# Where LayerNorm rows run and when filler steps are issued beside sliding-window attention

## The chip, the cores and the metric

One core of a Trainium2 chip runs the whole program. The metric is the device time of one execution in microseconds (us). The engines are TensorE (PE, its weight loads shown apart as PEld), VectorE (DVE), ScalarE (ACT), GpSimd (POOL), and SyncE (SP), on whose queue nearly all DMAs are issued.

## The reference

A transformer block whose two LayerNorms are modulated by a condition: sliding-window attention, then a dense network with the mish activation, each with a gated residual. All is fp32. There are 2048 tokens of width D = 448, 16 heads of Dh = 28, a window W = 256 and a hidden width F = 1792.

```python
mod = (silu(c) @ w_mod).reshape(1, 6, 1, 448)
sa, ca, ga, sb, cb, gb = (mod[:, i] for i in range(6))
h = layernorm(x) * (1 + ca) + sa
q, k, v = split_heads(h @ wqkv)                       # 16 heads of 28
scores = q @ k.T * 28 ** -0.5
mask = (i - j >= 0) & (i - j < 256)                   # query i, key j
o = softmax(where(mask, scores, -1e9)) @ v
x = x + ga * (merge_heads(o) @ wo)
h = layernorm(x) * (1 + cb) + sb
x = x + gb * (mish(h @ w1 + b1) @ w2)                 # mish: t * tanh(log1p(exp(t)))
```

## The kernel before

**Arithmetic.** An fp32 value that TensorE multiplies is split into a high part, written by ScalarE as a rounded copy, and a low part, the value minus that copy, written by VectorE or GpSimd. A product is then three matmuls: high with high, high with low and low with high.

**Tiling.** The tokens are cut into 4 groups (0 to 3) of 512. A group and a head make a slot, 64 in all (`s`), and a slot has three attention units (`BLOCKS`); the unit number `u` runs from 0 to 191, 48 to a group. A name such as `P58` in an order is that of unit 58.

**One unit of attention.** `B` puts the scores of keys against queries into a PSUM bank (`sB`, L709 and L720) and lets ScalarE take the exponential twice: `P` in fp32 (L723) and `Ph`, the high part (L724). `SP` lets GpSimd make the low part, `Pl` = P - Ph (L731). `PV` multiplies both by the values into `pv` (L741), `Ph` two units later and `Pl` three. The row maximum that the exponential needs comes earlier: `A` computes scores the other way round (`sA`, L679), VectorE reduces each to a maximum (`mx`, L681), and for each pair of slots `M2` turns the maxima and splits them (`mr`, L689 and L690), and a DMA adds them to the queries as further rows. `sA`, `sB`, `pv` and `mm` (for filler) have two PSUM banks each, P, Ph and Pl three buffers each.

**After attention.** `EV` copies a finished slot out of PSUM on ScalarE: `o` (L747) and `ol` (L749). For every four slots (a quad) `QA` adds the two on GpSimd, `T1` turns the sum on VectorE into `t4` and takes the reciprocal `rc` of the softmax denominators (L770), `TM` multiplies by it on GpSimd (L775), and `T2` turns the result back on VectorE into `on` (L779). When four quads are there, the group's output is complete and `on_full` holds the group.

**Filler.** Between the units of a group, `fill_main` issues work of neighbouring groups. In group g (for g over 0) it finishes the q and k projections of group g, waits until `on_full` holds group g-1, and issues `gen_oT` (high part of `on` on ScalarE, L621, low part on VectorE) and `gen_wo` (the output projection, with the residual and the statistics of LN2 behind it). Then `gen_hT` for group g+1 turns the normalized rows through TensorE (four turnings, `tr`), and modulates them into a high part (ScalarE) and a low part (VectorE), and `gen_qkv` projects them. How much of it goes to a unit is set by credit: each unit adds `RATE[g]`, and each filler step takes off what it yields (for matmuls about their share of time, for a turning a constant).

**Side work.** Once in a unit `side_step` advances a second list: above all LN1 of the next group (`gen_ln` with a key that begins with a: statistics `mva` on VectorE, `rsa`, 1 / sqrt(variance + eps), on GpSimd with L233 and L234, then four rows `xin` of 128 tokens, L240, with `dup` on GpSimd behind each), sums for the modulation, and loading of the FFN's weights. LN2 uses the same `gen_ln` with keys f0 to f3 and its rows, `x1`, on VectorE; f0 is issued in the last units of attention.

**Order.** The order on each engine is the order in which the program issues; each engine takes its instructions strictly in turn. `Pipe` holds back stages of a filler item: `add(hold, f1, f2)` calls f1 at the next step, f2 at the one after, and None stands for a step without work. `later` is a queue of DMAs, from which a step takes one at most. After the last unit (`u` = 192 and on) the FFN runs, with L923 (`z`) and L1114 to L1116 (`acc`) as its matmuls; it takes the span from about 440 us.

Of the kernel before, what the change touches and what calls it, by code (L numbers as in the profile page):

```python
# [51 lines left out]
def adaln_block(ctx: ExitStack, tc: tile.TileContext, x, wqkv, wo, w1, b1, w2, c, w_mod, out):  # L52
    nc = tc.nc
    PE, ACT, DVE, POOL = nc.tensor, nc.scalar, nc.vector, nc.gpsimd
# [36 lines left out]
    def bank(tag, bufs, name):  # L91
        return PS[0].tile([128, 512], F32, name=name, tag=tag, bufs=bufs)
# [32 lines left out]
    for part in range(3):  # L125
        for ci in range(4):
            r0, r1 = ci * 128, min(ci * 128 + 128, D)
            for h in ((slice(0, 128),) if ci < 3 else (slice(0, 64), slice(64, 128))):
                t = wqs[ci][h]
# [87 lines left out]
    def ln_stats(x, mv, pl, key):  # L217
        st = pl.tile([128, 6], F32, name=f"st{key}", tag="st", bufs=2)
        DVE.bn_stats(st, x)
        DVE.bn_aggr(mv, st)  # L220

    def dup(x):
        POOL.tensor_copy(x[:, D:512], x[:, 384:448])

    def gen_ln(tiles, pl, xn_tiles, key, mv=None):
        if mv is None:
            mv = pl.tile([128, 4, 2], F32, name=f"mv{key}", tag="mv", bufs=2)
            for t in range(4):
                ln_stats(tiles[t], mv[:, t, :], pl, f"{key}{t}")
                if t < 3:  # L230
                    yield
        rs = pl.tile([128, 4], F32, name=f"rs{key}", tag="rs", bufs=2)
        POOL.tensor_scalar(rs, mv[:, :, 1], EPS, None, op0=ALU.add)  # L233
        POOL.tensor_tensor(rs, rs, mhalf, op=ALU.pow)  # L234
        yield
        yield
        xs = xn_tiles()
        for t in range(4):
            xn = xs[t]
            (POOL if key[0] == "a" else DVE).tensor_scalar(xn[:, 0:D], tiles[t], mv[:, t, 0:1], rs[:, t:t + 1],  # L240
                                                           op0=ALU.subtract, op1=ALU.mult)
            if t:
                dup(xs[t - 1])
            yield xs
        dup(xs[3])

    def tr_chunk(xs, ci, p):
        for t in range(4):
            PE.transpose(p[:, t * 128:(t + 1) * 128], xs[t][:, ci * 128:(ci + 1) * 128], ident)  # L249
# [5 lines left out]
    def hT_hi(p, ci, hh, si):  # L255
        ACT.activation(hh[:, ci], p, AF.Identity, scale=cols[:, si + 1, ci:ci + 1], bias=cols[:, si, ci:ci + 1])

    def hT_lo(p, ci, hh, hl, si, y=True):
        if y:
            hT_y(p, ci, si)  # L260
        DVE.tensor_tensor(hl[:, ci], p, hh[:, ci].bitcast(F32), op=ALU.subtract)

    def new_T(key, pl):
        return (pl.tile([128, 4, GT], F32R, name=f"hh{key}", tag="hh"),
                pl.tile([128, 4, GT], F32R, name=f"hl{key}", tag="hl"))
# [17 lines left out]
    pipe = Pipe()  # L283
    ht_done = set()

    def gen_hT(g):
        drain(ln1[g])
        hh, hl = HT[g] = new_T(g, mid)
        for ci in range(4):
            p = bank("mm", 2, f"tr{g}{ci}")  # L290
            tr_chunk(XS[g], ci, p)
            pipe.add(2, lambda p=p, ci=ci: hT_hi(p, ci, hh, 0), lambda p=p, ci=ci: hT_lo(p, ci, hh, hl, 0))
            yield 1.2
        ht_done.add(g)
        if g + 1 < NG:
            loads = (lambda: x_load(g + 1),) if g > 1 else (lambda: (x_tile(g + 1), x_half(g + 1, 0)),
                                                            lambda: x_half(g + 1, 2))
            pipe.add(0, None, None, lambda: later.extend(loads))
# [5 lines left out]
    def drain(*gs):  # L304
        for g in gs:
            for _ in g:
                pipe.step()
# [17 lines left out]
    def flush():  # L325
        while later:
            later.pop(0)()
# [289 lines left out]
    def gen_oT(g, oT_pool):  # L617
        o = on[g]
        oh, ol = OT[g] = new_T(f"o{g}", oT_pool)
        for ci in range(4):  # L620
            ACT.activation(oh[:, ci], o[:, ci], AF.Copy)  # L621
            pipe.add(1, lambda ci=ci: DVE.tensor_tensor(ol[:, ci], o[:, ci], oh[:, ci].bitcast(F32), op=ALU.subtract))
            if ci < 3:
                later.append(lambda t=ci: xr_load(g, t))
            yield
        yield
        if g == NG - 1:
            yield
# [36 lines left out]
    NS = NG * H  # L665
# [78 lines left out]
    def EV(i, part):  # L744
        a = i % 4 * 32
        if part == 0:
            ACT.activation(O4[a:a + 32], pvb[i][0:32, :], AF.Copy)  # L747
        elif i < NS - 3:
            ACT.activation(OL4[a:a + DH], pvb[i][32:60, :], AF.Copy)  # L749
        else:  # L750
            DVE.tensor_copy(OL4[a:a + DH], pvb[i][32:60, :])

    def quad(qd):
        g, ci = divmod(qd, 4)
        if ci == 0 and g not in on:
            on[g] = mid.tile([128, 4, GT], F32, name=f"on{g}", tag="on")
        return on[g][:, ci], T4.rearrange("p (b d) -> p b d", d=32)
# [14 lines left out]
    def TM(qd):  # L772
        o, t = quad(qd)
        for eng, a, b in ((POOL, 0, 16),) if qd < NS // 4 - 1 else ((POOL, 0, 6), (DVE, 6, 16)):
            eng.tensor_tensor(t[:, a:b, 0:28], t[:, a:b, 0:28], rcq[qd][:, a:b].to_broadcast([128, b - a, 28]), op=ALU.mult)  # L775

    def T2(qd):
        o, t = quad(qd)
        DVE.transpose(o, T4)  # L779
        if qd % 4 == 3:  # L780
            on_full.add(qd // 4)
# [204 lines left out]
        if not (told.get(g) == "bank" and pipe.held() or told.get(g) in taken):  # L986
            told[g] = next(side[g], None)

    RATE = {0: 0.56, 1: 0.91, 2: 0.91, 3: 0.65}
    FRONT = {0: 0, 1: 2, 2: 2, 3: 2}  # L990
    ln1 = {g: gen_ln1(g) for g in range(1, NG)}
    fillers = {g: fill_main(g) for g in range(NG)}
# [2 lines left out]
    def step(g):  # L995
        return next(fillers[g], 99.0) or RATE[g]

# [37 lines left out]
    NU = 3 * NS  # L1035
    credit = 0.0
    for u in range(NU + 9):
        s, k = divmod(u, 3)
        g = s // H
        if k == 0 and s % H == 0 and 0 < g < NG:  # L1040
            drain(fillers[g - 1], side[g - 1])
            flush()
        pipe.step()
        if 0 <= u - 3 < NU:
            PV(u - 3, Pl)
            if k == 2 and s % 4 != 1:
                EV(s - 1, 0)
        if k == 0 and 0 <= s - 2 < NS:
            if s % 4 == 2:
                EV(s - 2, 0)  # L1050
            EV(s - 2, 1)
        qd = (s - 5) // 4
        if k == 1 and s % 4 == 1 and 0 <= qd < NS // 4:
            QA(qd)
        if u < NU:
            B(u)
        if 0 <= u - 1 < NU:
            SP(u - 1)
        a = s + LEAD
        if a < NS:  # L1060
            A(a, (0, 1, 3)[k])
        if k == s % 2 and s < NS:
            load_slot(s + LEAD + 2)
        if k == 2 and s % 4 == 1 and 0 <= qd < NS // 4:
            T1(qd)
            TM(qd)
        qd = (s - 6) // 4
        if k == (1 if u < NU else 0) and s % 4 == 2 and 0 <= qd < NS // 4:
            T2(qd)
        if g < NG:  # L1070
            v = u - 48 * g
            if v in (0, 12):
                chunk["v"] = 4 if v == 0 and g or 0 < g < NG - 1 else 2
            if v == 0:
                credit = 0.0
            credit += RATE[g] * (2 if v < FRONT[g] else 1)
            while credit > 0.0:
                credit -= step(g)
        if k == 0 and (a - 1) % 2 == 1 and LEAD <= a - 1 < NS:
            M2((a - 1) // 2)  # L1080
        if g < NG:
            if v > 1 or g == 0:
# [12 lines left out]
        if 0 <= u - 2 < NU:
            PV(u - 2, Ph)
# [53 lines left out]
    for n in range(NN + 1):  # L1150
        g, f = divmod(n, NF)
# [44 lines left out]
```

## Time and profile before

| | |
|---|---|
| time, median of 3 runs | 728.78 us (727.71 to 729.55) |
| the profiled execution | 728.02 us, of which 726.2 are the profile's span |
| mean granted TensorE clock | 0.979 |
| busy: PE, DVE, ACT, POOL | 689.5, 397.5, 422.5, 368.9 us |
| issued DMA data | 83.74 MB |

The span starts with the program's first instruction and ends with its last. A group's line gives: source line, engine and operation, output<-inputs, count, then busy time and the mean in ns of one, and behind the second bar the idle time of the engine just before these instructions with what ended it. In the timeline a line gives start, duration, engine, line, operation, and in brackets the wait and what released it. Names lose their numbers there: `P` is any unit's. The granted clock of 1.00 is full speed.

### The profile page before, as it was taken

What the parts mean: (1) busy time and instruction counts of PE and PEld (TensorE: products, weight loads), DVE (VectorE), ACT (ScalarE), POOL (GpSimd) and SP (SyncE); (2) the same over time, 40 slices, a digit from 0 to 9 for tenths busy, and PEclk for the clock granted to TensorE, in tenths of its full rate; (3) what the DMA queues carried; (4) which work ended last, traced back from release to release, by engine and by line L of the source; (5) the groups of instructions that cost most, each with busy time, mean ns of one, the idle gap of its engine ahead of it and who ended that gap; (6) DMA issues with size and microseconds to landing.
All of it is one profiled execution on the core that took longest, in us unless ns stands there. A gap on an engine that the chain in (4) does not pass through costs nothing. (4 is left out here: it accounts for less than half of the span.)

```text
span 726.2 us, 11790 instructions
## 1 busy us (share of the span) xinstructions
PE 689.5 (95%) x3873; PEld 586.1 (81%) x3873; DVE 397.5 (55%) x992; ACT 422.5 (58%) x772; POOL 368.9 (51%) x369
## 2 busy tenths in 40 slices
PE   8998999889999899999899899999999999999996
PEld 8776777678888687888687678888888888888885
DVE  5677767757765958676868776232324133323112
ACT  4549888768877868778978894334233222322221
POOL 7576888797765897677779847332010000000002
PEclk9999999989999999999989899999999999999999
DMA  7855863444482452664764155500200030001001
GB/s 217 258 200 176 247 200 116 137 132 158 135 261 68 150 181 95 171 193 124 227 189 129 52 172 158 141 14 1 101 1 1 0 102 1 0 1 51 0 1 51
DMA packets 48329, 83.74 MB, mean 115 GB/s; under 512 B 6286, under 2 KB 26428, under 8 KB 48268
## 3 DMA queue, kind: packets, MB, share of 16 engines
q1 hardware_dynamic: 47804, 82.98, 36.7%
q8 instruction: 31, 0.51, 0.3%
q14 instruction: 30, 0.25, 0.1%
q10 hardware_dynamic: 464, 0.00, 0.0%
HBM read 53.34 MB, written 29.36 MB: 114 GB/s over the span
## 5 line engine op out<-in xcount | busy, mean ns | idle before, releaser
L731 POOL TENSOR_TENSOR Pl<-P,Ph 128x512 fp32r<-128x512 f32 (+2 forms) x192 | 235.6, 1238 | 66.3 <-ACT Ph L724 39.1
L681 DVE CUSTOM_DVE_ANT_0 junk<-sA,mask 128x384 bf16<-128x384 f32 (+2 forms) x256 | 134.4, 525 | 93.6 <-PE sA L679 84.6
L929 ACT ACTIVATE t<-z,b1c 128x512 f32<-128x512 f32 x56 | 38.5, 687 | 190.5 <-PE z L923 187.4
L931 DVE TENSOR_TENSOR al<-t,ah 128x512 fp32r<-128x512 f32 x56 | 40.7, 726 | 188.3 <-ACT ah L930 188.3
L723 ACT ACTIVATE P<-sB 128x512 f32<-128x512 f32 (+2 forms) x192 | 110.0, 573 | 43.4 <-PE sB L720 36.1
L679 PE MATMUL sA<-k,q 84*128 84x384 f32 (+2 forms) x256 | 103.9, 408 | 8.2 <-DVE mx L681 5.2
L724 ACT ACTIVATE Ph<-sB 128x512 fp32r<-128x512 f32 (+2 forms) x192 | 109.3, 569 | 0.0
L923 PE MATMUL z<-hhf,w 128*128 128x512 f32 x224 | 89.4, 399 | 0.0
L741 PE MATMUL pv<-Pl,v 128*60 128x256 f32 (+2 forms) x352 | 76.7, 293 | 12.8 <-POOL Pl L731 12.0
L923 PE MATMUL z<-hlf,w 128*128 128x512 f32 x224 | 88.4, 395 | 0.0
L1115 PE MATMUL acc<-w2l,ah 128*128 128x448 f32 x224 | 81.6, 364 | 0.4 <-POOL w2l L893 0.4
L1114 PE MATMUL acc<-w2h,ah 128*128 128x448 f32 x224 | 81.8, 365 | 0.0
L1116 PE MATMUL acc<-w2h,al 128*128 128x448 f32 x224 | 81.7, 365 | 0.0
L741 PE MATMUL pv<-Ph,v 128*60 128x256 f32 (+2 forms) x352 | 79.2, 300 | 0.0
L709 PE MATMUL sB<-q,k 86*128 86x256 f32 (+1 forms) x352 | 76.8, 293 | 2.1 <-ACT Ph L724 1.4
L709 PEld LDWEIGHTS sB<-q,k 86*128 86x128 f32 x352 | 63.5, 196 | 5.1 <-ACT Ph L724 2.2
L923 PE MATMUL z<-hhf,w1l 128*128 128x512 f32 x168 | 66.3, 395 | 0.0
L741 PEld LDWEIGHTS pv<-Pl,v 128*60 128x60 f32 x352 | 45.4, 136 | 24.7 <-POOL Pl L731 18.3
L679 PEld LDWEIGHTS sA<-k,q 84*128 84x128 f32 x256 | 50.8, 200 | 15.5 <-DVE mx L681 9.2
L720 PE MATMUL sB<-fdmask,identr 128*128 128x128 bf16 (+1 forms) x320 | 61.7, 259 | 0.0
L1123 POOL TENSOR_TENSOR yo<-yo,x 128x448 f32<-128x448 f32 (+1 forms) x4 | 4.2, 1058 | 108.1 <-DVE yo L1120 108.1
L741 PEld LDWEIGHTS pv<-Ph,v 128*60 128x60 f32 x352 | 47.4, 137 | 14.3 <-issue 1.3
(155 smaller groups left out, 1337.0 us busy)
## 6 DMA issues: line engine op xcount, KB each, us to landing
scr<-st SPq DMA_DIRECT2D x24, 512.0 KB
k<-scr SPq DMA_DIRECT2D x48, 252.0 KB
q<-scr SPq DMA_DIRECT2D x64, 168.0 KB
scr<-st SPq DMA_DIRECT2D x32, 256.0 KB
x<-x1d SPq DMA_DIRECT2D x10, 448.0 KB
xin<-in_A_x_dram SPq DMA_DIRECT2D x8, 448.0 KB
xr<-in_A_x_dram SPq DMA_DIRECT2D x16, 224.0 KB
x1d<-xr SPq DMA_DIRECT2D x16, 224.0 KB
```

The costliest lines, as they stand in the source:

```text
L679: PE.matmul(p[:, c0:384], q[0:84, t * 128:(t + 1) * 128], k[0:84, t * 128 + c0:t * 128 + 384], start=True, stop=True)
L681: DVE.tensor_tensor_reduce(out=junk[:, c0:384], in0=p[:, c0:384], in1=mask[:, c0:384], scale=1.0, scalar=-3.0e38, op0=ALU.add, op1=ALU.max ...
L709: PE.matmul(p[:, c:c + 128 * (t1 - t0)], k[:, jj * 128:(jj + 1) * 128], q[:, t0 * 128:t1 * 128], start=(n == 0), stop=False, skip_group_ch ...
L720: PE.matmul(p[:, c:c + n], identr, fdmask[:, m:m + n], start=False, stop=True, skip_group_check=True)
L723: ACT.activation(P[:, c0:], p[:, c0:], AF.Exp, scale=SCALE)
L724: ACT.activation(Ph[u][:, c0:], p[:, c0:], AF.Exp, scale=SCALE)
L731: eng.tensor_tensor(Pl[u][:, a:b], Pt[u][:, a:b], Ph[u][:, a:b].bitcast(F32), op=ALU.subtract)
L741: PE.matmul(pv[0:60, t0 * 128:t1 * 128], V[j % NV][:, h, :], P[u][:, c:c + 128 * (t1 - t0)], start=(P is Ph and b == 0 and n == 0), stop=F ...
L923: PE.matmul(zb[n], ps[m][1], ps[m][0], start=(m == 0), stop=(m == 10))
L1114: PE.matmul(p, ah[n][:, ts], w2h[f], start=(f == 0), stop=False)
L1115: PE.matmul(p, ah[n][:, ts], w2l[f], start=False, stop=False)
L1116: PE.matmul(p, al[n][:, ts], w2h[f], start=False, stop=(f == NF - 1))
```

## The change

Five things change.

1. The rows of LN1 in groups 1 to 3 (`xin`, twelve of 128 x 448) are normalized by ScalarE as `Identity(rs * x + nm)` instead of by GpSimd as `(x - mean) * rs`. GpSimd makes the bias nm = -mean * rs with two more small operations behind `rsa`.
2. For the keys a1, a2, a3 and f0 the rows are issued one unit later (one more `yield`).
3. A turning in `gen_hT` takes 1.9 off the credit instead of 1.2, and the credit per unit grows: `RATE` from 0.56 to 0.64 in group 0, from 0.91 to 1.02 in groups 1 and 2.
4. The low part of `gen_oT` (VectorE) is issued one step later.
5. The division `TM` moves from behind `T1`, the third unit of its slot, to the first unit of the next slot, and `T2` from the second unit of that slot to the third.

```diff
         POOL.tensor_tensor(rs, rs, mhalf, op=ALU.pow)
+        if key[0] == "a":
+            nm = pl.tile([128, 4], F32, name=f"nm{key}", tag="nm", bufs=2)
+            POOL.tensor_scalar(nm, mv[:, :, 0], -1.0, None, op0=ALU.mult)
+            POOL.tensor_tensor(nm, nm, rs, op=ALU.mult)
         yield
         yield
+        if key in ("a1", "a2", "a3", "f0"):
+            yield
         xs = xn_tiles()
         for t in range(4):
             xn = xs[t]
-            (POOL if key[0] == "a" else DVE).tensor_scalar(xn[:, 0:D], tiles[t], mv[:, t, 0:1], rs[:, t:t + 1],
-                                                           op0=ALU.subtract, op1=ALU.mult)
+            if key[0] == "a":
+                ACT.activation(xn[:, 0:D], tiles[t], AF.Identity, scale=rs[:, t:t + 1], bias=nm[:, t:t + 1])
+            else:
+                DVE.tensor_scalar(xn[:, 0:D], tiles[t], mv[:, t, 0:1], rs[:, t:t + 1],
+                                  op0=ALU.subtract, op1=ALU.mult)
...
             pipe.add(2, lambda p=p, ci=ci: hT_hi(p, ci, hh, 0), lambda p=p, ci=ci: hT_lo(p, ci, hh, hl, 0))
-            yield 1.2
+            yield 1.9
...
             ACT.activation(oh[:, ci], o[:, ci], AF.Copy)
-            pipe.add(1, lambda ci=ci: DVE.tensor_tensor(ol[:, ci], o[:, ci], oh[:, ci].bitcast(F32), op=ALU.subtract))
+            pipe.add(2, None, lambda ci=ci: DVE.tensor_tensor(ol[:, ci], o[:, ci], oh[:, ci].bitcast(F32), op=ALU.subtract))
...
-    RATE = {0: 0.56, 1: 0.91, 2: 0.91, 3: 0.65}
+    RATE = {0: 0.64, 1: 1.02, 2: 1.02, 3: 0.65}
...
         if k == 2 and s % 4 == 1 and 0 <= qd < NS // 4:
             T1(qd)
-            TM(qd)
         qd = (s - 6) // 4
-        if k == (1 if u < NU else 0) and s % 4 == 2 and 0 <= qd < NS // 4:
-            T2(qd)
+        if s % 4 == 2 and 0 <= qd < NS // 4:
+            if k == 0:
+                TM(qd)
+            if k == (2 if u < NU else 0):
+                T2(qd)
```

In the changed kernel the lines of the attention stand nine further down (L723 becomes L732, L731 becomes L740); the rows are L247 on ScalarE and L249 on VectorE.

**ScalarE, early in group 1 (units 58 to 60).** `xin2` are rows of LN1 for group 2, `hho0` the high parts of group 0's attention output, `o4` and `ol4` a slot's copy out of PSUM. Before:

```order
L723 ACTIVATE P58_2137<-sB58_2133 128x512
L724 ACTIVATE Ph58_2138<-sB58_2133 128x512
L621 ACTIVATE hho0_2069<-on0_1026 128x512
L747 ACTIVATE o4_462<-pv18_2098 32x512
L723 ACTIVATE P59_2165<-sB59_2160 128x512
L724 ACTIVATE Ph59_2166<-sB59_2160 128x512
L749 ACTIVATE ol4_463<-pv18_2098 28x512
L723 ACTIVATE P60_2189<-sB60_2184 128x512
L724 ACTIVATE Ph60_2190<-sB60_2184 128x512
```

Now:

```order
L732 ACTIVATE P58_2139<-sB58_2135 128x512
L733 ACTIVATE Ph58_2140<-sB58_2135 128x512
L630 ACTIVATE hho0_2099<-on0_1020 128x512
L756 ACTIVATE o4_462<-pv18_2102 32x512
L732 ACTIVATE P59_2167<-sB59_2162 128x512
L733 ACTIVATE Ph59_2168<-sB59_2162 128x512
L630 ACTIVATE hho0_2099<-on0_1020 128x512
L247 ACTIVATE xin2_1114<-xin2_1114,nma2_2054,rsa2_2051 128x448
L758 ACTIVATE ol4_463<-pv18_2102 28x512
L732 ACTIVATE P60_2192<-sB60_2187 128x512
L733 ACTIVATE Ph60_2193<-sB60_2187 128x512
L247 ACTIVATE xin2_1114<-xin2_1114,nma2_2054,rsa2_2051 128x448
```

A high part of the attention output and the first row now stand between Ph59 and P60, and the second row between Ph60 and P61.

**GpSimd at the same place (units 53 to 57).** `t4` is the division of a quad, `Pl53` to `Pl57` the low parts of units 53 to 57. Before:

```order
L775 TENSOR_TENSOR t4_464<-t4_464,rc3_2008 128x16x28
L731 TENSOR_TENSOR Pl53_2037<-P53_1998,Ph53_1999 128x512
L233 TENSOR_SCALAR rsa2_2047<-mva2_1918 128x4
L234 TENSOR_TENSOR rsa2_2047<-rsa2_2047,mhalf_136 128x4
L731 TENSOR_TENSOR Pl54_2063<-P54_2033,Ph54_2034 128x512
L731 TENSOR_TENSOR Pl55_2092<-P55_2059,Ph55_2060 128x512
L731 TENSOR_TENSOR Pl56_2114<-P56_2088,Ph56_2089 128x512
L240 TENSOR_SCALAR xin2_1100<-xin2_1100,mva2_1918,rsa2_2047 128x448
L731 TENSOR_TENSOR Pl57_2141<-P57_2110,Ph57_2111 128x512
```

Now:

```order
L740 TENSOR_TENSOR Pl53_2040<-P53_2006,Ph53_2007 128x512
L784 TENSOR_TENSOR t4_464<-t4_464,rc3_2016 128x16x28
L233 TENSOR_SCALAR rsa2_2051<-mva2_1922 128x4
L234 TENSOR_TENSOR rsa2_2051<-rsa2_2051,mhalf_136 128x4
L237 TENSOR_SCALAR nma2_2054<-mva2_1922 128x4
L238 TENSOR_TENSOR nma2_2054<-nma2_2054,rsa2_2051 128x4
L740 TENSOR_TENSOR Pl54_2069<-P54_2036,Ph54_2037 128x512
L740 TENSOR_TENSOR Pl55_2093<-P55_2065,Ph55_2066 128x512
L740 TENSOR_TENSOR Pl56_2117<-P56_2089,Ph56_2090 128x512
L740 TENSOR_TENSOR Pl57_2143<-P57_2113,Ph57_2114 128x512
```

The division stands behind Pl53 instead of ahead of it, two operations on 4 elements stand ahead of Pl54, and no row stands ahead of Pl57.

**VectorE late in group 3 (LN2 of group 0 begins).** `mx62` are row maxima of slot 62, `mr30` the turned and split maxima of an earlier pair, `x1_0` a row of LN2 (`rsf0` its 1 / sqrt), `w13` a weight's low part, `on3` a turned quad. Before:

```order
L681 ISA junk_479,mx62_5573<-sA62_0_5574,mask_153 128x384
L681 ISA mx62_5573 128x1
L240 TENSOR_SCALAR x1_0_5227<-x1_0_5227,mv2_0_475,rsf0_5552 128x448
L689 CAST mr30_5579<-sA61_3_5549 8x128
L690 TENSOR_TENSOR mr30_5579<-sA61_3_5549,mr30_5579 8x128
L199 TENSOR_TENSOR w13_5051<-w1p3_5144,w13_5051 64x448
L681 ISA junk_479,mx62_5573<-sA62_1_5599,mask_153 128x384
```

Now:

```order
L788 STREAM_TRANSPOSE on3_5100<-t4_464 128x512
L690 ISA junk_479,mx62_5582<-sA62_0_5583,mask_153 128x384
L690 ISA mx62_5582 128x1
L698 CAST mr30_5587<-sA61_3_5557 8x128
L699 TENSOR_TENSOR mr30_5587<-sA61_3_5557,mr30_5587 8x128
L199 TENSOR_TENSOR w13_5059<-w1p3_5152,w13_5059 64x448
L690 ISA junk_479,mx62_5582<-sA62_1_5607,mask_153 128x384
L690 ISA mx62_5582 128x1
L249 TENSOR_SCALAR x1_0_5236<-x1_0_5236,mv2_0_475,rsf0_5561 128x448
```

The row of LN2 stands behind the maxima of the next score tile instead of ahead of `mr30`, and a transposition has come ahead of the first maximum.

## The prediction

> **What bounds the kernel now.** I read the page first, then 5 us windows, the waits, the groups, and last the timeline at the worst places.
>
> ```profile
> PE 689.5 (95%) x3873; PEld 586.1 (81%) x3873; DVE 397.5 (55%) x992; ACT 422.5 (58%) x772; POOL 368.9 (51%) x369
> ```
>
> TensorE is busy 95% of the span: its 36.7 us without work, and the stretches at a lower granted clock, are all that a reordering can win. From the windows I keep those in which the clock falls (columns: stretch, its length, busy PE, PEld, DVE, ACT, POOL, then the granted clock):
>
> ```profile
> 45.00:50.00 5.00, 5.00 (x30) 4.11 (x29) 3.58 (x12) 2.19 (x6) 5.00 (x8) 1.00 0.65 225
> 140.00:145.00 5.00, 3.28 (x22) 2.10 (x21) 4.96 (x11) 4.90 (x10) 4.92 (x6) 1.00 0.90 287
> 145.00:150.00 5.00, 3.02 (x18) 1.97 (x17) 4.12 (x13) 4.93 (x10) 5.00 (x3) 0.92 0.32 94
> 150.00:155.00 5.00, 4.88 (x19) 4.21 (x20) 0.57 (x2) 1.28 (x3) 5.00 (x6) 0.50 0.92 293
> 155.00:160.00 5.00, 5.00 (x32) 4.49 (x31) 2.99 (x9) 3.75 (x7) 5.00 (x5) 0.90 0.31 97
> 245.00:250.00 5.00, 3.44 (x20) 2.64 (x20) 5.00 (x11) 4.90 (x10) 4.92 (x6) 0.82 0.81 265
> 250.00:255.00 5.00, 3.24 (x20) 2.72 (x18) 4.09 (x13) 4.52 (x10) 5.00 (x3) 0.84 0.42 115
> 255.00:260.00 5.00, 4.90 (x23) 4.42 (x24) 1.07 (x4) 2.24 (x5) 5.00 (x6) 0.66 0.92 311
> 360.00:365.00 5.00, 4.08 (x20) 3.37 (x17) 4.77 (x13) 4.48 (x9) 3.33 (x4) 0.58 0.84 269
> 365.00:370.00 5.00, 5.00 (x27) 4.44 (x26) 2.60 (x8) 2.42 (x5) 3.19 (x3) 0.74 0.46 123
> 400.00:405.00 5.00, 4.06 (x21) 3.25 (x22) 4.76 (x13) 2.41 (x5) 4.44 (x5) 0.68 0.01 2
> 405.00:410.00 5.00, 5.00 (x30) 4.45 (x29) 2.71 (x11) 4.11 (x8) 2.97 (x4) 0.64 0.03 7
> ```
>
> There are four slow spells. In each, TensorE first waits for a third of the time or more, then runs at about half its clock. The loss is 5 us times the missing clock: 5 x (0.08 + 0.50 + 0.10) = 3.4 us at 145 to 160, 5 x (0.18 + 0.16 + 0.34) = 3.4 at 245 to 260, 5 x (0.42 + 0.26) = 3.4 at 360 and 5 x (0.32 + 0.36) = 3.4 at 400: 13.6 us in all. The first two spells are the places where LN1 of groups 2 and 3 is normalized and attention's output is turned over to the projection; GpSimd is full there, and ScalarE is full until 150.
>
> ```profile
> PE pv L741 <- POOL Pl L731: 12.0, 15, 1.9
> POOL t L775 <- DVE rc L770: 9.5, 9, 2.2
> PE sA L679 <- DVE mr L690: 2.0, 1, 2.0
> PE sA L679 <- DMA k<-scr: 0.6, 1, 0.6
> ```
>
> TensorE's largest wait is on `Pl`, the low part that GpSimd makes for each unit of attention. The timeline shows why at 150 (GpSimd, then TensorE):
>
> ```profile
> 140.84 1.05 POOL L234 TENSOR_TENSOR rsa<-rsa,mhalf 128x4 f32<-128x4 f32 x1
> 141.86 4.63 POOL L731 TENSOR_TENSOR Pl<-P,Ph 128x512 fp32r<-128x512 f32 x3
> 146.48 2.35 POOL L240 TENSOR_SCALAR xin<-xin,mva,rsa 128x448 f32<-128x448 f32 x1
> 148.81 2.49 POOL L731 TENSOR_TENSOR Pl<-P,Ph 128x512 fp32r<-128x512 f32 x2
> 143.18 0.45 PE L741 MATMUL pv<-Pl,v 128*60 128x128 f32 x2 [1.14 <-POOL Pl L731]
> 150.12 0.68 PE L741 MATMUL pv<-Pl,v 128*60 128x128 f32 x2 [1.82 <-POOL Pl L731]
> 255.10 0.68 PE L741 MATMUL pv<-Pl,v 128*60 128x128 f32 x2 [1.85 <-POOL Pl L731]
> ```
>
> One LN row of 2.35 us stands ahead of Pl57; TensorE waits 1.82 us for it, and 1.85 us at the same place of the next group.
>
> **The change, part by part.** The sum is made against the profiled execution, 728.02 us (span 726.2 and 1.8 around it); the median of the runs, 728.78, lies 0.76 above it.
>
> ```profile
> L240 POOL TENSOR_SCALAR xin<-xin,mva,rsa 128x448 f32<-128x448 f32 x12 | 23.2, 1936 | 0.1
> L406 ACT ACTIVATE xin<-xin,rs 128x448 f32<-128x448 f32 x4 | 2.7, 750 | 3.6 <-DVE rs L411 3.6
> L233 POOL TENSOR_SCALAR rsa<-mva 128x4 f32<-128x4 f32 x3 | 0.7, 231 | 8.9 <-DVE mva L220 8.9
> L234 POOL TENSOR_TENSOR rsa<-rsa,mhalf 128x4 f32<-128x4 f32 x3 | 3.1, 1042 | 0.2
> L747 ACT ACTIVATE o<-pv 32x512 f32<-32x512 f32 x64 | 37.3, 583 | 22.8 <-PE pv L741 22.4
> L749 ACT ACTIVATE ol<-pv 28x512 f32<-28x512 f32 x61 | 35.9, 589 | 1.3
> ```
>
> *LN rows off GpSimd.* Twelve rows of 1.94 us (23.2 us) leave GpSimd. The four of group 1 lie before the first unit, where ScalarE has 2.8 us of every 5 free (the window 45 to 50): nothing either way. In groups 2 and 3 the row ahead of Pl57 goes, and with it waits of 1.82 and 1.85: **-3.7 us**. The Trainium skill's GPSIMD Engine Reference (section 4.1, Engine selection) holds that GpSimd runs one-input elementwise work at about line rate, which with the 1.03 cycles per element of its section 3.1 would be an estimated 0.4 us for a row. By that the wait removed would be 0.4 twice, and the sum 2.9 us poorer; the trace's 1936 ns disagrees, and it decides.
>
> *LN rows onto ScalarE.* A row takes 0.75 us there (norm0, the same operation on the same shape). Two of the four now stand ahead of P61, in a stretch in which ScalarE is already busy 9.83 of 10 us; the other two come where projection matmuls fill TensorE. Queued behind the first two are ol4, P60, P61 and what GpSimd and TensorE make of them. Since sB and pv have two banks, TensorE can be two units ahead, so I count half of 1.5 us. GpSimd gets two small operations between rsa and Pl54; the first is like L233 (0.23), the second lies between that and L234 (1.04); I take 0.23, since no power is in it. Pl54 already makes TensorE wait 1.14, so all of that 0.5 counts. Together 1.25 per group: **+2.5** (0 to 2 x (1.5 + 1.27) = 5.5).
>
> *The clock.* Whether a slow spell goes depends on whether the waits ahead of it shrink enough. In groups 1 and 2 one wait of two goes, at 400 the one that is named next. I let two of four go: 6.8 us. Part of that time lies under ScalarE, which is busy 4.48 of 5 at 360 to 365 and would set the pace itself; I take **-5.0** (0 to -13.6).
>
> *The LN2 rows a step later.* At 398 VectorE's first x1 row stood ahead of mr30:
>
> ```profile
> 398.61 1.45 DVE L240 TENSOR_SCALAR x<-x,mv,rsf 128x448 f32<-128x448 f32 x1 [0.64 <-POOL rsf L234]
> 400.62 0.19 PEld L679 LDWEIGHTS sA<-k,q 84*128 84x128 f32 x1 [2.28 <-DVE mr L690]
> L779 DVE STREAM_TRANSPOSE on<-t 128x512 f32<-128x512 f32 x16 | 11.3, 705 | 0.4 <-POOL t L775 0.4
> ```
>
> It waited 0.64 us for rsf and ran 1.45, while TensorE waited 2.0 for mr. Now mr30 goes first, but the transposition of 0.7 us has come ahead of sA62_0. I take 2.0 less 0.3: **-1.7** (-2.0 to -1.3). The last turning moves one unit nearer to the first FFN matmul; TensorE is still held by ScalarE's exponentials there, so nothing.
>
> *Division, transposition and low parts a step later.* GpSimd no longer waits for the reciprocal ahead of a Pl (9.5 us of waiting in 9 places), VectorE no longer for the division or for hho. Of TensorE's 12.0 us on Pl, 3.7 are counted above and about 2.3 belong to Pl54, so 6.0 are left to win; most of the 9.5 is slack, since GpSimd is only half busy overall. **-1.0** (0 to -6.0). Behind the later low parts stands wo0, which starts one unit later; that is in the next term. On SP's queue loads of xr, wm and x1d change places with loads of q and k; TensorE waits 0.6 us on such a load in the whole run, so nothing, and about that much again if the cover fails.
>
> *Spaced turnings and the faster filler.* A turning now counts 1.9 instead of 1.2, and the projection is finished sooner. Counting in the order: the gap without projection matmuls is units 53 to 60 instead of 54 to 59, the units 46, 47, 94 and 142 are empty now, and each of three turnings takes two more thin units: 4 + 4 + 6 = 14 more thin units.
>
> ```profile
> L709 PEld LDWEIGHTS sB<-q,k 86*128 86x128 f32 x352 | 63.5, 196 | 5.1 <-ACT Ph L724 2.2 <-ACT P L723 1.0 <-issue 0.6
> L741 PEld LDWEIGHTS pv<-Pl,v 128*60 128x60 f32 x352 | 45.4, 136 | 24.7 <-POOL Pl L731 18.3 <-DVE Pl L731 0.5
> L741 PEld LDWEIGHTS pv<-Ph,v 128*60 128x60 f32 x352 | 47.4, 137 | 14.3 <-issue 1.3
> L679 PEld LDWEIGHTS sA<-k,q 84*128 84x128 f32 x256 | 50.8, 200 | 15.5 <-DVE mx L681 9.2 <-DVE mr L690 2.9 <-DMA q<-scr 1.0
> L720 PEld LDWEIGHTS <-identr 128*128 128x128 bf16 x320 | 21.5, 101 | 10.7 <-issue 2.0
> 139.31 0.60 ACT L723 ACTIVATE P<-sB 128x512 f32<-128x512 f32 x1
> 140.28 0.60 ACT L723 ACTIVATE P<-sB 128x512 f32<-128x512 f32 x1
> ```
>
> In a thin unit TensorE's weight loads are the pace: (63.5 + 45.4 + 47.4 + 50.8 + 21.5) / 192 = 1.19 us. ScalarE needs 0.97 for P and Ph (139.31 to 140.28, back to back) and a third of o and ol, 0.39: 1.36. Each thin unit leaves TensorE 0.17 us idle: 14 x 0.17 = **+2.4** (0, if run-ahead hides it, to 14 x 0.39 = 5.5, if o and ol fall due at once).
>
> The sum: -3.7 + 2.5 - 5.0 - 1.7 - 1.0 + 2.4 = -6.5, that is 721.5 for the profiled execution and **722.3** on the median.
>
> **The rivals.**
>
> *The clock stays.* The waits shrink, but all four spells stay: ScalarE, full up to 150, holds TensorE back as long as GpSimd did. For it: ScalarE's 9.83 of 10. Against: after 150 it is idle while TensorE runs at half clock. The sum without the clock is -1.5: 727.3, no measurable change. Chance 0.14, with that of the moves merely cancelling.
>
> *All slow spells go.* Then the clock gives 13.6 instead of 5.0: -15.1, 713.7. For it: the spells follow on waits, and the largest is taken away in three of the four places. Against: ScalarE-bound units leave TensorE idle anyhow. Chance 0.13. The Trainium skill's TensorE: Matmul & The Clock Gate ("Why this matters for your kernels") says that the clock falls after idle gaps above some 3 us; by that no spell would be left. The trace disagrees as it stands: the spells come with no single wait above 2.28 us.
>
> *Slower: the gap becomes ScalarE's.* Rows on a full ScalarE and a later Pl54 take the place of the wait removed. Then nothing is won on Pl (0), the added wait stands at its upper end (+5.5), no spell goes, mr30 gives -1.7, the thin units +2.4: +6.2, 735.0. It decides from the point where TensorE waits more than 1.14 + 1.82, some 3 us, for Pl54 and for P60 and P61 together. For it: the 9.83 of 10, and rsa must now wait for statistics that VectorE has moved behind a low part of st. Against: half of the rows fall past the gap. Chance 0.18.
>
> **How the numbers follow.** The forecast of 722.3 has 0.55, and its own range is 718.5 to 726. Faster or slower by over 0.3% (2.2 us, about what a measurement of this kernel can tell) then come to: faster 0.55 + 0.13 = 0.68, same 0.14, slower 0.18. The range leaves the slower rival out, takes in the other two, and reaches past no change for its milder forms: 713 to 730.5.
>
> **What would show it.** Right: PE's wait on Pl falls from 12.0 to about 8; no wait of 1.8 ahead of the first wo matmul; the granted clock at 1.00 in at least two of the four places; no wait on mr of 2 us. Wrong: ACT rows xin ahead of P60 with TensorE waiting on Ph or P right behind; a wait of 2 us or more on Pl54; new windows with a clock under 1.00, at the turnings above all.

## Result: no measurable change

The changed kernel takes 727.65 us (median of 12 runs, 725.03 to 731.68), the kernel before 728.03 in the same comparison. The ratio is 0.9995 with a 95% interval of 0.9975 to 1.0014. The forecast was 722.3. That the range of 713 to 730.5 held the time is luck: it reached that far for the milder forms of a rival. The forecast change, 6.5 us, did not come. The profiled execution took 729.9 us, 728.1 of it span, so it lies 2.3 above the median.

The page, busy time by engine; ScalarE has 7 us more than before, GpSimd 20 less, TensorE the same:

```profile
PE 688.9 (95%) x3873; PEld 582.3 (80%) x3873; DVE 399.7 (55%) x992; ACT 429.5 (59%) x784; POOL 348.7 (48%) x363
```

The waits (total, times, longest):

```profile
POOL rsa L233 <- DVE mva L220: 11.3, 3, 9.0
PE pv L750 <- POOL Pl L740: 8.4, 12, 2.1
PE sA L688 <- DMA k<-scr: 5.1, 4, 2.2
PE sA L688 <- DVE mx L690: 4.0, 4, 1.6
POOL t L784 <- DVE rc L779: 3.2, 1, 3.2
```

TensorE's wait on `Pl` fell from 12.0 to 8.4 us and GpSimd's on `rc` from 9.5 to 3.2, as the change meant. New are the wait of `rsa` for the statistics (three instead of one) and TensorE's on keys that a DMA brings (5.1 instead of 0.6).

The windows of 5 us, with the granted clock behind the engines' busy times:

```profile
105.00:110.00 5.00, 3.68 (x14) 3.23 (x15) 1.46 (x5) 2.50 (x7) 3.17 (x3) 0.66 0.54 160
145.00:150.00 5.00, 2.86 (x18) 2.23 (x19) 2.77 (x9) 3.17 (x6) 4.08 (x6) 0.76 0.98 313
150.00:155.00 5.00, 5.00 (x27) 4.34 (x25) 3.70 (x10) 3.80 (x8) 4.44 (x4) 0.56 0.41 144
215.00:220.00 5.00, 4.62 (x19) 4.11 (x20) 1.79 (x6) 1.60 (x4) 3.01 (x3) 0.66 0.51 189
250.00:255.00 5.00, 3.39 (x21) 2.80 (x20) 4.59 (x15) 4.00 (x8) 3.33 (x4) 0.84 0.72 229
255.00:260.00 5.00, 3.74 (x17) 2.92 (x15) 2.36 (x8) 3.66 (x7) 4.48 (x7) 0.50 0.91 313
360.00:365.00 5.00, 4.73 (x36) 3.71 (x35) 4.04 (x11) 4.47 (x9) 2.82 (x3) 1.00 0.47 112
400.00:405.00 5.00, 4.31 (x29) 3.03 (x28) 4.76 (x13) 4.88 (x11) 4.83 (x5) 1.00 0.03 10
```

The slow spells of 360 and 400 are gone. Those of 150 and 255 stayed, with 3.4 us of missing clock each as before, and two shorter ones came, at 107 and 217, with 1.7 each.

What TensorE waits for ahead of the spell at 147 is in the timeline. Before, on VectorE, the last statistics stand ahead of `st`, the low part of a q and k projection:

```profile
139.37 0.62 DVE L219 BATCH_NORM_STATS2 sta<-xin 128x6 f32<-128x448 f32 x1
140.03 0.18 DVE L220 BATCH_NORM_AGGREGATE mva<-sta 128x2 f32<-128x6 f32 x1
140.14 0.69 DVE L338 TENSOR_TENSOR st<-qk,st 128x512 fp32r<-128x512 f32 x1
```

In the changed kernel `st` stands ahead of the maximum and of the statistics (VectorE, then GpSimd, then TensorE):

```profile
143.68 0.69 DVE L347 TENSOR_TENSOR st<-qk,st 128x512 fp32r<-128x512 f32 x1
144.29 0.55 DVE L690 CUSTOM_DVE_ANT_0 junk<-sA,mask 128x384 bf16<-128x384 f32 x1
144.76 0.62 DVE L219 BATCH_NORM_STATS2 sta<-xin 128x6 f32<-128x448 f32 x1
145.42 0.18 DVE L220 BATCH_NORM_AGGREGATE mva<-sta 128x2 f32<-128x6 f32 x1
145.69 0.24 POOL L233 TENSOR_SCALAR rsa<-mva 128x4 f32<-128x4 f32 x1 [1.14 <-DVE mva L220]
146.01 1.04 POOL L234 TENSOR_TENSOR rsa<-rsa,mhalf 128x4 f32<-128x4 f32 x1
147.12 0.24 POOL L237 TENSOR_SCALAR nma<-mva 128x4 f32<-128x4 f32 x1
147.45 0.20 POOL L238 TENSOR_TENSOR nma<-nma,rsa 128x4 f32<-128x4 f32 x1
147.60 3.72 POOL L740 TENSOR_TENSOR Pl<-P,Ph 128x512 fp32r<-128x512 f32 x3
144.90 0.44 PE L688 MATMUL sA<-k,q 84*128 84x384 f32 x1 [1.58 <-DVE mx L690]
148.92 0.68 PE L750 MATMUL pv<-Pl,v 128*60 128x128 f32 x2 [2.14 <-POOL Pl L740]
106.32 0.41 PE L718 MATMUL sB<-q,k 86*128 86x384 f32 x1 [1.72 <-ACT ol L758]
215.38 0.42 PE L688 MATMUL sA<-k,q 84*128 84x384 f32 x1 [2.20 <-DMA k<-scr]
```

GpSimd stands still for 1.14 us at `rsa`, and Pl54 waits behind it: TensorE waits 1.58 us for the maximum and then 2.14 for Pl54. The wait of 1.82 on Pl57 is gone; this took its place, three units earlier. The last two rows are the waits ahead of the spells at 107 and 217.

### The profile page after: what moved, and what is told of

Read it like the earlier page. It is cut to its first block, busy times and chain, and to the rows that moved or that the text cites. A ratio compares the mean times of both kernels' runs of the same rounds, so it can differ in the third digit from the quotient of the medians.

```text
span 728.1 us, 11809 instructions
## 1 busy us (share of the span) xinstructions
PE 688.9 (95%) x3873; PEld 582.3 (80%) x3873; DVE 399.7 (55%) x992; ACT 429.5 (59%) x784; POOL 348.7 (48%) x363
## 4 chain that ended last, share of the span: by engine, by line
PE 65%; issue 12%; DVE 7%; ACT 6%; DMA 6%; POOL 2%; SPq 1%; POOLq 0%; DVEq 0%; ACTq 0%
PE z L932 14%; PE pv L750 8%; PE qk L323 7%; PE wo L323 5%; PE acc L1126 4%; PE acc L1127 4%; PE acc L1125 4%; PE sA L688 4%; PE sB L718 4%; PE qk_v L323 3%; PE sB L729 3%; DMA scr<-st 2%; DMA k<-scr 2%; ACT Ph L733 2%; DVE junk L690 2%
## 5 line engine op out<-in xcount | busy, mean ns | idle before, releaser
L740 POOL TENSOR_TENSOR Pl<-P,Ph 128x512 fp32r<-128x512 f32 (+2 forms) x192 | 234.1, 1226 | 95.1 <-ACT Ph L733 60.2
L938 ACT ACTIVATE t<-z,b1c 128x512 f32<-128x512 f32 x56 | 38.5, 687 | 192.0 <-PE z L932 188.9
L732 ACT ACTIVATE P<-sB 128x512 f32<-128x512 f32 (+2 forms) x192 | 110.1, 573 | 36.9 <-PE sB L729 32.4
L688 PE MATMUL sA<-k,q 84*128 84x384 f32 (+2 forms) x256 | 100.4, 400 | 9.5 <-DMA k<-scr 5.1
L1126 PE MATMUL acc<-w2l,ah 128*128 128x448 f32 x224 | 81.6, 364 | 0.4 <-POOL w2l L902 0.4
L718 PEld LDWEIGHTS sB<-q,k 86*128 86x128 f32 x352 | 62.0, 194 | 10.6 <-ACT Ph L733 5.3
```

What stands on the lines that cost most here:

```text
L688: PE.matmul(p[:, c0:384], q[0:84, t * 128:(t + 1) * 128], k[0:84, t * 128 + c0:t * 128 + 384], start=True, stop=True)
L718: PE.matmul(p[:, c:c + 128 * (t1 - t0)], k[:, jj * 128:(jj + 1) * 128], q[:, t0 * 128:t1 * 128], start=(n == 0), stop=False, skip_group_ch ...
L732: ACT.activation(P[:, c0:], p[:, c0:], AF.Exp, scale=SCALE)
L740: eng.tensor_tensor(Pl[u][:, a:b], Pt[u][:, a:b], Ph[u][:, a:b].bitcast(F32), op=ALU.subtract)
L1126: PE.matmul(p, ah[n][:, ts], w2l[f], start=False, stop=False)
```

## The experiments

Sixteen kernels in four comparisons, each beside runs of the kernel before; "ratio" is against it, with the 95% interval. The experiments are mostly set against e1, whose six runs spread over 9.3 us, so a difference from e1 of under about 3 us isn't clear of noise (estimated from the spread of the runs on both sides). Part numbers are those of the change: 1 rows on ScalarE, 2 one more unit for a1 to a3 and f0, 3 turnings at 1.9 and the new RATE, 4 low part of `gen_oT` later, 5 TM and T2 later.

### Part 3 against the others: e1 to e4

e1, the changed kernel without part 3:

```diff
-    RATE = {0: 0.64, 1: 1.02, 2: 1.02, 3: 0.65}
+    RATE = {0: 0.56, 1: 0.91, 2: 0.91, 3: 0.65}
-            yield 1.9
+            yield 1.2
```

> The changed kernel with part 3 undone (credit of a turning 1.2 and the old RATE); parts 1, 2, 4 and 5 stay. Theory A (the faster filler gives the gain back: its waits on k and on the statistics of LN1, and the clock spells behind them, come from part 3): PE's wait for DMA k falls from 5.1 to about 0.6 us, POOL rsa no longer waits for mva in groups 2 and 3, no low clock near 107 and 217, and the time falls to 720 to 724. Rival B (the rows on ScalarE and the longer chain on GpSimd ahead of Pl54 hold the gap): the waits of 2.14 and 1.26 on Pl and of 1.6 on mx stay, and the time stays at 726 to 729.

719.12 us, ratio 0.9888 (0.9853 to 0.9924). Theory A held, with a time 0.9 us below its range: parts 1, 2, 4 and 5 are worth 8.8 us. In its profile TensorE waits less on `Pl` and on k, `rsa` hardly waits, and there is no slow spell in attention at all (waits, then GpSimd and TensorE in the timeline):

```profile
PE pv L750 <- POOL Pl L740: 6.4, 8, 1.5
PE sA L688 <- DMA k<-scr: 1.5, 2, 0.8
140.43 0.24 POOL L233 TENSOR_SCALAR rsa<-mva 128x4 f32<-128x4 f32 x1 [0.26 <-DVE mva L220]
141.49 0.44 PE L688 MATMUL sA<-k,q 84*128 84x384 f32 x1 [0.25 <-DVE mx L690]
143.68 0.45 PE L750 MATMUL pv<-Pl,v 128*60 128x128 f32 x2 [1.50 <-POOL Pl L740]
```

The wait for the maximum is 0.25 instead of 1.58 us, that on Pl54 1.50 instead of 2.14.

e2, the kernel before with part 3 alone (the same four lines, the other way):

> The kernel before with part 3 alone (a turning counts 1.9, the new RATE). Theory A: slower, 731 to 735, with PE waiting 4 to 5 us for DMA k. Rival B: within 2 us of the kernel before.

736.57 us, ratio 1.0120 (1.0100 to 1.0141): part 3 alone costs 8.6 us, more than theory A's range, with only 2.7 us of waiting for k. The two add up: -8.8 + 8.6 = -0.2, and the whole change measured -0.4.

e3, the changed kernel with the old RATE and turnings at 1.9:

> The changed kernel with the old RATE but turnings still at 1.9: splits part 3. If the credit of the turnings makes the k projections late, PE's wait for DMA k stays at 5 us or grows, and the time is 728 to 733, since the slower filler has nothing to catch up with. If the new RATE is what hurts (a low part of st pulled ahead of the last statistics on VectorE), rsa no longer waits for mva and the time is 722 to 725.

726.50 us, ratio 0.9987 (0.9973 to 1.0002). Neither guess held: the time is between them. `rsa` hardly waits, and TensorE doesn't wait for k but for `q<-mr`, in group 0 (e16 below).

e4, the changed kernel with the extra yield ahead of `rs`, so that `rsa` and `nma` come one unit later and the rows stay:

```diff
+        if key in ("a1", "a2", "a3", "f0"):
+            yield
         rs = pl.tile([128, 4], F32, name=f"rs{key}", tag="rs", bufs=2)
...
         yield
         yield
-        if key in ("a1", "a2", "a3", "f0"):
-            yield
```

> The changed kernel with the extra yield of part 2 put ahead of rs instead of behind it: rsa and nma stand one unit later on GpSimd, the rows where they were. Theory A': the Pl54 waits (2.14 and 1.26 us) come from rsa standing ahead of Pl54 and waiting for mva; they fall under 0.5 each, the two low-clock spells at 147 and 255 shrink, 722 to 725. Rival B: ScalarE and VectorE hold the gap anyway (PE waits for mx 1.6 us); nothing beyond 1 us, 726.5 to 728.

725.86 us, ratio 0.9972 (0.9956 to 0.9988). In the changed kernel the place of `rsa` costs 1.8 us of the 8.5, though the two intervals overlap. The time is above the range of theory A', and the waits didn't fall under 0.5: TensorE now waits 1.2 us one unit later in each group, behind the same small operations (group 1):

```profile
148.61 0.45 PE L750 MATMUL pv<-Pl,v 128*60 128x128 f32 x2 [1.21 <-POOL Pl L740]
```

### The other half of part 3, and parts 1, 5 and 2 one by one: e5 to e8

e5, the changed kernel with turnings back at 1.2 and the new RATE kept:

> The changed kernel with turnings back at 1.2 but the new RATE kept: the other half of part 3. Theory A1 (the loss is the turnings' 1.9, which makes the next group's q and k late): 719 to 722, no wait for DMA k above 0.6 us. Theory A2 (the loss is the new RATE, by rsa waiting for mva at Pl54 in groups 2 and 3): rsa waits 1.1 us twice as in the changed kernel, Pl waits of 2.1 and 1.3 stay, 723 to 726.

728.16 us, ratio 1.0006 (0.9984 to 1.0027), above both ranges; `rsa` waits as A2 said, and TensorE 2.1 us on Pl54. So in the changed kernel the new RATE is the cost: beside it the turnings' 1.9 changes nothing (727.65), although it brings the 5.1 us of waiting for k. The group start looks as in the changed kernel:

```profile
144.36 0.24 POOL L233 TENSOR_SCALAR rsa<-mva 128x4 f32<-128x4 f32 x1 [1.08 <-DVE mva L220]
```

e6, e1 without part 1 (the rows are on GpSimd, at the place to which part 2 puts them, and `nm` is gone):

```diff
-            if key[0] == "a":
-                ACT.activation(xn[:, 0:D], tiles[t], AF.Identity, scale=rs[:, t:t + 1], bias=nm[:, t:t + 1])
-            else:
-                DVE.tensor_scalar(...)
+            (POOL if key[0] == "a" else DVE).tensor_scalar(...)
```

> The changed kernel without part 3 (e1) and without part 1: LN1's rows on GpSimd again, without nma; parts 2, 4 and 5 stay. If the rows on ScalarE carry the gain of e1 (728 to 719), this is 725 to 728, with PE's wait on Pl ahead of the first wo matmul back at 1.8 us in groups 2 and 3. By the prediction's terms (rows -3.7 + 2.5 and part of the clock) it is 721 to 723. If moving them is neutral, 719 to 720.

725.58 us, ratio 0.9970 (0.9955 to 0.9985): 6.5 us more than e1. As in the kernel before, each row of a group stands ahead of a `Pl`, but one unit later; there TensorE waited over a us behind one of the four, here behind three (its timeline, then the total of that wait, then one of the rows on GpSimd):

```profile
151.76 0.45 PE L743 MATMUL pv<-Pl,v 128*60 128x128 f32 x2 [1.05 <-POOL Pl L733]
155.01 0.44 PE L743 MATMUL pv<-Pl,v 128*60 128x128 f32 x2 [1.14 <-POOL Pl L733]
164.01 0.45 PE L743 MATMUL pv<-Pl,v 128*60 128x128 f32 x2 [1.57 <-POOL Pl L733]
PE pv L743 <- POOL Pl L733: 13.1, 15, 1.6
151.70 1.85 POOL L242 TENSOR_SCALAR xin<-xin,mva,rsa 128x448 f32<-128x448 f32 x1
```

The 6.5 us are thus the price of rows on GpSimd at the later place, not where the kernel before had them; e11 is the test of that.

e7, e1 without part 5 (TM right behind T1, T2 at the second unit, as before):

> e1 without part 5: division TM and transposition T2 at their old steps. By the prediction (-1.0 for parts 4 and 5 together) 719.5 to 720.5. Rival: the wait of GpSimd on rc (9.5 us in 9 places before, 3.2 in 1 after) stood in front of Pl, and part 5 carries most of e1's gain: 723 to 726, with POOL t waiting for DVE rc 8 to 10 us again.

718.76 us, ratio 0.9868 (0.9848 to 0.9887): as e1. GpSimd waits for `rc` again, and TensorE's wait on `Pl` is back near the 12.0 us of before, yet the time is the same:

```profile
POOL t L784 <- DVE rc L779: 12.1, 10, 2.0
PE pv L750 <- POOL Pl L740: 11.9, 15, 1.8
```

A total of waits is thus no price. Why these waits cost nothing wasn't tested; that the next wait would have come in their place is a guess.

e8, e1 with f0 out of the list of part 2:

> e1 without the later rows of LN2's first group (key f0 out of the list of part 2); a1 to a3 stay. By the prediction's term of 1.7 us: 720.5 to 722, with PE waiting some 2 us for DVE mr near the end of attention. Rival (the wait is refilled by ScalarE, which is full there): 718.5 to 719.5.

722.31 us, ratio 0.9932 (0.9909 to 0.9955): f0 a unit later is worth 3.2 us, at the edge of the noise. Without it the wait on `mr` is back, and in this profile the clock falls there:

```profile
PE sA L688 <- DVE mr L699: 1.9, 1, 1.9
390.00:395.00 5.00, 3.09 (x14) 2.32 (x14) 4.51 (x9) 2.97 (x6) 5.00 (x5) 0.77 0.01 2
```

### Parts 4, 2 and 1 again, and a better version: e9 to e12

e9, e1 with `pipe.add(1, ...)` for the low part of `gen_oT`, as before:

> e1 without part 4: the low part of gen_oT one step earlier again. By the prediction (1.0 for parts 4 and 5 together, and e7 gave nothing for part 5): 719.5 to 720.5. Rival: in group 3 units 12 to 36 took 47.5 us before, 42.2 in e1 and still 44.2 without f0 (e8); part 5 gave 0.8 of the rest, so part 4 carries some 2.5 us there: 721.5 to 723, with that stretch at 44.5 to 45.

721.51 us, ratio 0.9921 (0.9893 to 0.9949). By the medians part 4 is worth 2.4 us, inside the rival's range but not clear of noise, and not where the rival said: the stretch of group 3 took 43.5 us, not 44.5, and the first 12 units of groups 1 and 2 took 1.2 to 1.4 longer, with slow spells in them that e1's profile lacks.

e10, e1 with f0 alone in the list (rows on ScalarE one unit earlier):

> e1 without the extra yield for a1 to a3 (f0 keeps it): the rows run on ScalarE one unit earlier, two of them in the gap in which ScalarE is full. If ScalarE is what holds the gap, each of two rows of 0.76 us in two groups costs about its length: 720.5 to 722. If TensorE's run-ahead hides them, as the small waits of e1 let one think: 718.5 to 719.5.

719.75 us, ratio 0.9898 (0.9873 to 0.9923): 0.6 from e1, inside the spread, though above the second guess. There is no sign that ScalarE holds the gap.

e11, the kernel before with part 1 alone and no extra yield:

> The kernel before with part 1 alone (rows on ScalarE, nma on GpSimd, no extra yield). If part 1 is worth by itself what e6 shows it to be worth beside the others (6.5 us): 721 to 722.5, no row ahead of Pl and no wait of 1.8 us at 150 and 255. By the prediction's terms (rows -1.2 and a share of the clock) 723 to 726. If it needs the other parts: 726 to 728.

723.02 us, ratio 0.9938 (0.9919 to 0.9957): 4.4 us below 727.39, the kernel before in this comparison. That is in the range of the prediction's terms and a share of the clock, but the terms came out otherwise. The wait on Pl57 is gone, and in its place TensorE waits longer than before on Pl54, behind `rsa` and `nma`; in group 2 the wait is again 2.28:

```profile
145.48 0.49 PE L748 MATMUL pv<-Pl,v 128*60 128x128 f32 x2 [2.28 <-POOL Pl L738]
```

Units 0 to 12 don't get shorter (27.8 and 28.0 us against 27.5 and 27.4). The gain lies in units 12 to 36, 49.0 in both groups against 52.0 and 52.1. In group 1 most of it, 2.4 us, is in units 60 and 61 (5.74 us before, 3.35 here), where TensorE was busy before but its granted clock was 0.50 and 0.90 in the windows from 150 to 160; in group 2 half of it, 1.6 us, is in units 108 and 109, at 0.66.

e12, e1 with the later `rsa` of e4:

> e1 with rsa and nma one unit later on GpSimd, behind Pl54 (as e4, without part 3). TensorE's wait on Pl54 in groups 1 and 2 (1.50 us at 143.68 in e1) goes: 717 to 718.5. If ScalarE takes it over (P waits, 1.25 us behind it in e1): 719, no change.

720.89 us, ratio 0.9914 (0.9888 to 0.9939): no gain where `rsa` hardly waits. TensorE's wait didn't go; it came one unit later, with 1.52 us. The best versions stay e7 and e1, 1.1 to 1.3% faster than both kernels; they can't be told apart.

### Where part 3 costs: e13 to e16

e13: e1 with 1.02 in groups 1 and 2 alone. e14: e1 with 0.64 in group 0 alone. e15: e13 with the later `rsa` of e4. e16: e1 with 1.9 for the turnings that group 0 issues:

```diff
-            yield 1.2
+            yield 1.9 if g == 1 else 1.2
```

> e1 with the new RATE in groups 1 and 2 alone (1.02), turnings at 1.2. If the wait of rsa for the statistics at Pl54 is the cost of the RATE: units 0 to 12 of groups 1 and 2 take 28.5 to 29.5 us instead of 26.4 and 26.8, in all 723 to 725. If the cost lies in group 0: 719 to 720.5.

> e1 with the new RATE in group 0 alone (0.64). If group 0 pays for the faster filler (units 12 to 36 took 40.9 us in e5, 38.6 in e1): 721 to 722.5. If that was one profile's chance: 718.5 to 720.

> e13 with rsa and nma one unit later on GpSimd. If rsa's wait is all that the RATE costs in groups 1 and 2: 719 to 721, the level of e12. If the emptier units around it cost by themselves: within 1.5 us of e13.

> e1 with the turnings' 1.9 in group 0 alone. 14 projection matmuls are then issued at once at the end of group 0, as in e3. If that is what e3 loses: 723 to 726, with group 0 at 80 to 82 us against 76.7. If e3 loses by its turnings in groups 1 and 2: 719 to 721.

| | us | ratio (95% interval) | against e1 |
|---|---|---|---|
| e13 RATE, groups 1 and 2 | 726.12 | 0.9973 (0.9955 to 0.9992) | +7.0 |
| e14 RATE, group 0 | 721.93 | 0.9923 (0.9899 to 0.9946) | +2.8 |
| e15 as e13, `rsa` later | 723.51 | 0.9934 (0.9911 to 0.9958) | +4.4 |
| e16 1.9, group 0 | 725.22 | 0.9956 (0.9941 to 0.9971) | +6.1 |

e13 and e14 add up to 9.8, e5 measured 9.0; e14's +2.8 by itself is not clear of noise. From the starts of `P` in each profile comes the length of a stretch in us (units counted within the group):

| | group 0 | 1: 0-12 | 12-36 | 36-48 | 2: 0-12 | 12-36 | 36-48 | 3: 12-36 |
|---|---|---|---|---|---|---|---|---|
| before | 77.1 | 27.5 | 52.0 | 25.1 | 27.4 | 52.1 | 25.1 | 47.5 |
| changed | 81.5 | 28.6 | 49.1 | 29.1 | 29.6 | 49.2 | 24.8 | 42.3 |
| e1 | 76.7 | 26.4 | 49.2 | 26.2 | 26.8 | 49.3 | 25.0 | 42.2 |
| e6 | 76.9 | 25.3 | 54.0 | 25.8 | 25.8 | 53.8 | 25.0 | 42.3 |
| e13 | 75.1 | 28.9 | 49.6 | 26.8 | 29.2 | 49.7 | 25.6 | 42.4 |
| e14 | 79.3 | 27.6 | 49.1 | 25.7 | 26.8 | 49.3 | 25.0 | 42.3 |
| e15 | 77.2 | 26.5 | 49.9 | 26.5 | 27.1 | 49.9 | 26.0 | 42.2 |
| e16 | 81.6 | 26.8 | 49.6 | 26.2 | 27.6 | 49.0 | 25.0 | 42.3 |

Each row is one execution, with its slow spells in it, so it shows where the time lies more than how much a part costs. By it the changed kernel keeps 11 us of gain against the kernel before (units 12 to 36 of groups 1, 2 and 3) and loses about as much in group 0 and in the outer stretches of groups 1 and 2.

In e13 the first 12 units of groups 1 and 2 grow by 2.5 and 2.4 us and the other four stretches of these groups by 0.4 to 0.6, 7.0 together; group 0 is 1.7 shorter. The two that grow hold a slow spell each, which e1's profile doesn't have, so the growth can't be split into waits and clock (the spell of group 1):

```profile
135.00:140.00 5.00, 3.42 (x23) 2.86 (x21) 4.61 (x16) 4.06 (x9) 3.13 (x5) 0.87 0.79 241
140.00:145.00 5.00, 3.86 (x19) 3.00 (x18) 2.21 (x8) 3.60 (x7) 4.78 (x6) 0.50 0.98 340
145.00:150.00 5.00, 5.00 (x28) 4.31 (x27) 4.44 (x11) 4.19 (x9) 3.24 (x3) 0.60 0.37 116
```

The later `rsa` takes the growth of these two stretches back, the spells lack 1.7 us of clock each instead of 5.2, and 2.6 us of the time go. The RATE in groups 1 and 2 thus costs 7.0 us with `rsa` at its place (e1 to e13) and 2.6 with `rsa` a unit later (e12 to e15): some 4.4 of the 7.0 seem to hang on that place, with some 4 us of noise on this difference of differences. What e15 keeps is the wait for the maximum, behind the same `st` on VectorE (TensorE):

```profile
141.27 0.44 PE L688 MATMUL sA<-k,q 84*128 84x384 f32 x1 [1.57 <-DVE mx L690]
244.50 0.44 PE L688 MATMUL sA<-k,q 84*128 84x384 f32 x1 [1.60 <-DVE mx L690]
```

In e1 it was 0.25 and 0.27. These waits aren't what e15 still loses: the stretches in which they lie are only 0.1 and 0.3 us longer than in e1. What is left lies in most of the others, 0.3 to 1.0 in each, and stays open. e16 loses most of its 6.1 us in group 0 (81.6 against 76.7). There the slower filler doesn't get through by the boundary, and 14 projection matmuls are issued at once in the last unit. Before that TensorE waits for one slot's maxima to come by DMA:

```profile
114.75 0.41 PE L718 MATMUL sB<-q,k 86*128 86x384 f32 x1 [3.00 <-DMA q<-mr]
```

In the changed kernel the longest wait on `q<-mr` is 0.5 us, and that backlog isn't there: its higher RATE pays for the dearer turnings. This fits the two halves of part 3 costing 7 to 9 us each and both together no more, but doesn't prove it, since group 0 of the changed kernel takes 81.5 us too, with other waits (1.72 at 106) and the spell at 107. With the higher RATE alone (e14) group 0 takes 79.3, and its units 12 to 36 take 40.7 us against 38.5 in e1, as expected; the kernels with the old RATE and 1.2 lie between 75.1 and 78.5 for the group. Why stays open.

## Why the prediction was wrong

The step that failed is *spaced turnings and the faster filler*. It was put at +2.4, with 5.5 as its upper end, and measured +8.5 (e1 against the changed kernel). Its price was that of emptier units alone, 0.17 us of TensorE's idle time for each. That price was not too low where it can be read: in e5 the six units without filler at the end of group 0 take 1.27 us each (from the start of P of unit 42 at 119.4 to that of unit 48 at 127.0), 0.08 above the 1.19 of TensorE's loads. What it left out is that the filler's own products move too. With 1.02 for two units in one, the first unit of a group issues all 11 matmuls of a projection instead of 8, so `st` reaches VectorE a unit earlier, ahead of the statistics and the maximum. The prediction had seen this, but only as a support for the slower rival, and gave it no term. The runs show in its place: the RATE in groups 1 and 2 costs 7.0 us (e13), by the medians 4.4 of them only while `rsa` stands ahead of Pl54 (e12, e15); in group 0 it costs perhaps 2.8 (e14); and the turnings' 1.9 without it costs 7.4 (e3), most of it in group 0 (e16). How much of each is waiting and how much is clock stays open.

Point by point:

- *Rows to ScalarE*: -3.7 + 2.5 = -1.2 predicted; -6.5 beside the others, against rows a unit later (e6), -4.4 alone (e11). Right in sign, too small, and not by the waits named. The GpSimd half of the +2.5 did come as a wait, on Pl54, of 1.50 us in e1 and 2.28 in e11 instead of 1.14; the ScalarE half left no measurable trace (e10). In e11 the gain lies behind these places, in units 12 to 36, into which the slow spells of the kernel before reach. So this term and that of the clock can't be told apart.
- *LN2 rows later*: -1.7 predicted, -3.2 measured (e8). Right in kind; the wait on `mr` is gone, and no slow spell follows there.
- *Division, transposition and low parts*: -1.0 predicted; part 4 is worth 2.4 by the medians (e9), part 5 nothing measurable (e7).
- *The clock*: -5.0 predicted. Two of the four spells went, as forecast, and two half as long came: 10.2 us of missing clock instead of 13.6. Over all runs the granted clock is 0.983 in both kernels, so the changed one got nothing from it. In e1, with 0.991, it would be over a third of the gain at the slope given below.
- *The rivals*: the one that ended slower had the right place, Pl54 behind `rsa`, and the named sign, "a wait of 2 us or more on Pl54", came true with 2.14. Its cause, a full ScalarE, was wrong: ScalarE is busy 3.17 of 5 us at 145 to 150. "The clock stays" gave the right time, 727.3, by luck: two spells did go, and the moves cancelled, but as 8.8 against 8.5.

The price of a row on GpSimd was rightly taken from the trace: in e6 a row takes 1.85 us, and all twelve take 23.2, as before; moving them away is worth 4.4 (e11) to 6.5 (e6). By the estimate of 0.4 us a row from the Trainium skill's GPSIMD Engine Reference (section 4.1, Engine selection, with section 3.1) all twelve rows would be 4.8 us of GpSimd's time; here too the trace disagrees.

## What to carry to other kernels

When a change alters how fast filler is issued, follow the filler's products on the other engines, not only the slots it leaves: a low part that comes a unit earlier can stand ahead of a statistic that something else is waiting for. Change the rate apart from the moves, since several good moves together can be hidden by one bad constant. Test a change of order beside the wait that comes next: in e11 the wait removed at Pl57 came back at Pl54. Price a wait by what comes next when it goes, not by its total: e7 put 5.5 us of waiting on `Pl` back and cost nothing, while e6 put back 6.7 and cost 6.5.

## What the hardware showed

The missing clock of a slow spell comes in steps. In all eighteen profiles here each spell ahead of 705 us lacks, by its windows of 5 us, about 1.7 us of clock or two or three times that: 3.4 four times in the kernel before, 1.7 and 3.4 twice each in the changed one, 5.2 twice and 1.7 in e13.

Run by run, time went with less than the clock that was missing. Over the 150 runs of the changed kernel and the experiments, a run with 0.001 more mean granted clock was 0.41 us shorter than others of the same kernel (standard error 0.04). If time went with the clock it would be 0.73. For the kernel before, the four comparisons give 0.04 to 0.22 us per 0.001. The prediction's "5 us times the missing clock" took the full price. From 0.983 to 0.991 the slope of 0.41 gives an estimated 3.3 of e1's 8.8 us.

The clock depends on the run as well as on the program: e1's runs range from 0.985 to 0.997 and from 714.87 to 724.15 us. Ahead of the new spells at 107 and 217 no matmul waited longer than the 2.20 us at 215.38. So the Trainium skill's rule (TensorE: Matmul & The Clock Gate, "Why this matters for your kernels"), by which gaps above some 3 us drop the clock, does not foretell these spells.
